# Chunk 0 of two attention backwards in 16 visits of three key blocks, and one weight fetch in five parts

## The chip, the cores and the metric

One NeuronCore of a Trainium2 chip runs the whole program. The metric is device time in microseconds (us), the median of several runs. Its engines are called as in the profile: PE (TensorE, matrix products and transposes), PEld (its weight loads), DVE (VectorE), ACT (ScalarE), POOL (GpSimd) and SP (SyncE, which issues every DMA of this kernel). Each engine works through its own instruction list in order.

## The reference: what is computed

Four layers on an x of 2048 rows by 640 columns in bfloat16: linear attention (A), sliding-window attention (B), A, B, with the same two weight sets used twice, and then the gradients of the whole chain.

```python
x = A_x
x = x + _A_ref(_layernorm(x, axis=-1), A_wqkv, A_wo)
x = x + _B_ref(_layernorm(x, axis=-1), B_wqkv, B_wo)
x = x + _A_ref(_layernorm(x, axis=-1), A_wqkv, A_wo)
x = x + _B_ref(_layernorm(x, axis=-1), B_wqkv, B_wo)
```

The outputs are x and the gradients of A_x, A_wqkv, A_wo, B_wqkv and B_wo. B has 32 heads of 20 columns and a causal window of 256 rows:

```python
scores = jnp.einsum("bhqd,bhkd->bhqk", q, k) * (Dh ** -0.5)
mask = (idx[:, None] - idx[None, :] >= 0) & (idx[:, None] - idx[None, :] < W)
p = _softmax(jnp.where(mask[None, None], scores, -1e9), axis=-1)
```

The change lies in the backward of B, for layer 3 and for layer 1.

## The kernel before

The program runs in passes: the forward of all layers, the backward of layer 3 (B), of layer 2 (A), of layer 1 (B), of layer 0 (A), and products for the weight gradients that are spread over the end. A pass is written out by hand: the order of the calls in Python is the order on PE, DVE, ACT and POOL, and in the two B backwards on SP too.

**Chunks, slabs and visits.** `core` (L1382) does a B backward in eight chunks of 256 query rows (two tiles of 128). A chunk has four slabs (`qr`, eight heads each), loaded by `core_loads` (L1341): slabT and slabqT (transposed k, v and q) and slabks and slabqs (k and q by rows). slabqT and slabqs have two buffers each. A slab has two halves (`p`), and `core_visits` (L708) cuts the blocks of a half into three visits. A block is one pair of a query tile and a key tile, 128 by 128, for one group of heads, two heads at a time. Chunks 1 to 7 have twelve blocks in a half, four in each visit. Chunk 0 has no keys before it and only six blocks, so two in each visit; 24 visits in every chunk.

**What a visit does.** `core_visit` (L759) works on four visits at once, six deep (`st.lag`): for visit n it forms the scores s on PE and e = exp(s) on ACT (L788) and masks e on POOL (L803 for two diagonal blocks in one instruction, L807 for one block); for visit n-3 it forms dp on PE and ds = dp * e on DVE (L792); for visit n-4 it transposes ds on PE (L814) and copies it out as dsT on ACT (L819) or DVE (L821); for visit n-6 `core_acc` accumulates on PE and, in the last visit of a half, the sums leave on ACT (L873, L881) and DVE. Ahead of the transposes of ds stand a number of transposes of the identity, whose result nobody reads (`warm`, L218), called warm-ups here: eight or nine in chunk 0 and five in chunk 1 by the list `thin`. s and dp have one PSUM tile each: the next s waits for e, the next dp for ds.

**What is laid between.** Each visit has two places for a piece of other work. `plan_before` prepares the next chunk (loads gb and ob, transposes gb on PE at L207, multiplies by WoTB, folds on POOL at L921 and L923, transposes into dT at L941). Its times are in a unit of which 32 make 24 visits; the chunk before gives it the room. `plan_behind` finishes a chunk two chunks later and first reads the tile WTB there, and WoTA after it. `hooks` are calls at the start of a visit, hook k at visit int(0.75 k); in layer 3 the first seven hold the end of the forward, hook 20 fetches WTB (the transposed qkv weights of B, 2400 KB) and hook 40 WoTA (800 KB). Layer 1 reads the same two tiles again.

**SP.** `put` hands a DMA over with a delay in visits, and `tick` issues what is due; the delays only set the order on SP. At run time SP issues the next DMA as soon as the one before is issued and its own data and buffer are free. In the first visit of each slab the loads of its slabks and slabqs are handed over with delay 1, and slabqT and slabT of the next slab with 1.1 and 1.3, so the order on SP is slabks, slabqs, slabqT, slabT.

Of the kernel before, what the change touches and what calls it, by code (L numbers as in the profile page):

```python
# [16 lines left out]
D = 640  # L17
# [58 lines left out]
class Kern:  # L76
# [119 lines left out]
            else:  # L196
                self.after(i, first)

    def fetch(self, w, src):
        self.dma(w.rearrange("p a b -> p (a b)"), src)  # L200

    def flip(self, ps, sb, src, name, w, n, step, eng, cols=None, **kw):

# [504 lines left out]
    def core_visits(self, st, l, S, c, qr, dq):  # L708

        t0 = 2 * c  # L710
        w0 = max(t0 - 2, 0)
        for p in range(2):
            if c == 0:
                order = [[(0, 0), (1, 0), (1, 1)]] * 2
            else:
                order = [[(0, 0), (0, 1), (1, 1), (0, 2), (1, 2), (1, 3)], [(0, 0), (0, 1), (0, 2), (1, 2), (1, 3), (1, 1)]]
            units = [(gi, bi, kk) for gi in range(2) for bi, kk in order[gi]]
            m = len(units) // 3
            for v in range(3):
                class U:  # L720
                    pass
                u = U()
                u.c, u.qr, u.p, u.S, u.dq, u.t0, u.w0, u.m = c, qr, p, S, dq, t0, w0, m
                u.blocks = units[v * m:(v + 1) * m]
                u.runs = []
                for j, (gi, bi, kk) in enumerate(u.blocks):
                    if u.runs and u.runs[-1][0:2] == [gi, bi] and u.runs[-1][2] + u.runs[-1][4] == kk and w0 + kk != t0:
                        u.runs[-1][4] += 1
                    else:
                        u.runs.append([gi, bi, kk, j, 1])  # L730
                u.first, u.last = v == 0, v == 2
                u.n = 24 * c + 6 * qr + 3 * p + v
                u.by_dma = self.by_dma(u.n)
                yield u

# [6 lines left out]
    def order(n):  # L742

        return ("FPA", "PFA", "PAF", "FAP", "AFP", "APF")[PLACES["fo"][n % 24] if 48 <= n < 192 else 0]

    WARM = (8, 5)
    TAIL = 5

# [10 lines left out]
    def core_visit(self, st, l, u, piece, on_act, thin):  # L759

        nc = self.nc
        h = st.hist
        h.append(u)

        def back(n):
            return h[-1 - n] if len(h) > n else None
        d, f, a = back(3), back(4), back(st.lag)
        pairs = []
        if d is not None:
            assert all(R["ok"] == at for R, at in d.S["ring"])  # L770
            d.dp = st.pD.tile([P, 2, 512], F32, name="dp")
            pairs.append(self.core_pairs(d, d.dp, lambda gi, bi: d.S["dT"][bi][:, 2 * d.qr + gi, :], "vT"))
        if u is not None:
            s = st.pS.tile([P, 2, 512], F32, name="s")
            pairs.append(self.core_pairs(u, s, lambda gi, bi: u.S["qT"][:, bi, gi, :], "kT"))
        if len(pairs) == 2:
            x, y = pairs
            while x or y:
                for z in (x, y):
                    if z:  # L780
                        z.pop(0)[1]()
        elif pairs:
            for _, z in pairs[0]:
                z()
        if u is not None:
            w = u.m * P
            u.e = st.pe.tile([P, 2, 4 * P], BF, name="e")
            nc.scalar.activation(u.e[:, :, 0:w], s[:, :, 0:w], ACT.Exp)  # L788
        if d is not None:
            w = d.m * P  # L790
            d.ds = st.pd.tile([P, 2, 4 * P], BF, name="ds")
            nc.vector.tensor_tensor(out=d.ds[:, :, 0:w], in0=d.dp[:, :, 0:w], in1=d.e[:, :, 0:w], op=ALU.mult)  # L792
            d.dsT = st.pt.tile([P, 8, P], BF, name="dsT")
            if d.by_dma:
                self.put(14, d.dsT, d.ds.rearrange("p j k -> p (j k)"), transpose=True)
        if u is not None:
            eb = u.e.rearrange("p j (k q) -> p j k q", q=P)
            for far in (0, 1):
                js = [j for j, (gi, bi, kk) in enumerate(u.blocks) if u.w0 + kk == u.t0 + bi - 2 * far]
                kw = dict(compare_op=ALU.is_ge, fill=0.0, base=-far, channel_multiplier=-1 if far else 1)  # L800
                if js == [0, 2]:
                    v = u.e.rearrange("p j (k q) -> p (j k) q", q=P)[:, 0:8:2, :]
                    nc.gpsimd.affine_select(out=v, in_=v, pattern=[[0, 4], [1 if far else -1, P]], **kw)  # L803
                    continue
                for j in js:
                    v = eb[:, :, j, :]
                    nc.gpsimd.affine_select(out=v, in_=v, pattern=[[0, 2], [1 if far else -1, P]], **kw)  # L807
        def flip_ds():
            ps = st.ps.tile([P, 8, P], BF, name="flip", tag="m")
            if thin:  # L810
                self.warm(thin, ps)
            for j in range(2):
                for i in range(f.m):
                    nc.tensor.transpose(ps[:, 4 * j + i, :], f.ds[:, j, i * P:(i + 1) * P], self.ident)  # L814

            def v(t):
                return t.rearrange("p (a b) q -> p a b q", a=2)[:, :, 0:f.m, :]
            if on_act:
                nc.scalar.copy(v(f.dsT), v(ps))  # L819
            else:  # L820
                nc.vector.tensor_copy(v(f.dsT), v(ps))  # L821
        parts = dict(F=None if f is None or f.by_dma else flip_ds, P=piece[0], A=None if a is None else lambda: self.core_acc(st, l, a))
        self.tick(0.5)
        for k in self.order(len(h) - 1):
            if parts[k] is not None:
                parts[k]()
        if piece[1] is not None:
            piece[1]()
        self.tick(0.5)
# [552 lines left out]
    def core(self, st, l, g_out, B, hooks):  # L1382
# [3 lines left out]
        plan = []  # L1386
        dq = {}
        for c in range(1, NC):
            plan += [(32 * (c - 1) + a, *f) for a, *f in self.plan_before(st, l, c, B)]
        for c in range(NC):  # L1390
            plan += [(32 * (c + 2) - (16 if c == NC - 1 else 0) + a, *f)
                     for a, *f in self.plan_behind(st, l, c, dq, g_out)]
        nv = 24 * NC + st.lag
# [7 lines left out]
        for n in range(48):  # L1401
            thin[n] = PLACES[f"ws{l}"][n] if n < 12 else self.WARM[n // 24]
        for n in range(168, nv):
            thin[n] += PLACES["tt"][n - 168]
        on_act = [PLACES["xx"][n % 24] for n in range(nv)]
        n = 0
        with ExitStack() as es:
            st.pS = self.pool(es, "pS", 1, bass.MemoryType.PSUM, "right")
            st.pD = self.pool(es, "pD", 1, bass.MemoryType.PSUM, "right")
            st.hist = []  # L1410
            for c in range(NC):
                for qr in range(4):
                    S = B.slabs.pop(0)
                    for i, u in enumerate(self.core_visits(st, l, S, c, qr, dq)):
                        for k, f in enumerate(hooks):
                            if int(k * 0.75) == n:
                                f()
                        if i == 0:
                            S["late"]()
                        if i == 0 and 4 * c + qr + 1 < 4 * NC:  # L1420
                            B.slabs.append(self.core_loads(l, *divmod(4 * c + qr + 1, 4), B))
                        if n == st.lag:
                            st.pA = self.psum(es, "pA", 1)
                            dqp = self.pool(B.dqs, "dqp", 3, side="right")
                        if n % 24 == st.lag:
                            dq[c] = dqp.tile([P, 2, QT], BF, name="dq")
                        self.core_visit(st, l, u, slots[n], on_act[n], thin[n])
                        n += 1
            for _ in range(st.lag):
                self.core_visit(st, l, None, slots[n], on_act[n], thin[n])  # L1430
                n += 1
# [14 lines left out]
    def passes(self):  # L1446
# [5 lines left out]
        st = S()  # L1452
        with ExitStack() as rest:
# [9 lines left out]
            hooks = tail[:-1] + [lambda: (tail[-1](), switch())] + [lambda: None] * (7 - n3)  # L1463

            hooks += [lambda: None] * (70 - len(hooks))
            hooks[20] = lambda: self.fetch(st.WTB, self.WT["B"])
            hooks[40] = lambda: self.fetch(st.WoTA, self.WoT["A"])
            left3 = self.core(st, 3, self.gs[2], st.core, hooks)
            for f in left3[:8]:
                if f is not None:  # L1470
# [10 lines left out]
            lp, B = self.linear_pools(lw, "left", 0), S()  # L1481
# [8 lines left out]
            plan = [(a, lambda f=f: f and f()) for a, f in enumerate(left3)] + [(20, next_pools)]  # L1490
# [16 lines left out]
            hooks = self.slots([(a - 20, f) for a, f, *_ in fs if a >= 20], 8)  # L1507
# [60 lines left out]
            with ExitStack() as es, ExitStack() as le:  # L1568
# [8 lines left out]
                X, plan = {}, []  # L1577
# [79 lines left out]
```

## Time and profile before

| | us |
|---|---|
| median of three runs | 2156.81 |
| lowest and highest run | 2153.57 and 2165.6 |
| profiled execution, first to last instruction | 2161.7 |
| TensorE busy in it | 2022.5 (94%) |
| VectorE, ScalarE, GpSimd busy | 1396.7, 1313.6, 1034.4 |

The profiled execution has no time of its own beside its span; the span lies within the three timed runs. In the lines further down a group reads: line of the kernel, engine, operation, tiles written and read, count, busy time and mean of one instruction, and idle time ahead with what ended it. In a line of the timeline the first two numbers are the start and the duration in us, and the bracket holds the idle time before it and its releaser. For a DMA on SP the duration is that of the issue; the time to landing is listed apart.

### The profile page before, as it was taken

Reading aid. Unit: us, or ns where it says so; the run is one execution under the profiler, and the core shown is the slowest. Engines: PE = TensorE matmul, PEld = TensorE weight load, DVE = VectorE, ACT = ScalarE, POOL = GpSimd, SP = SyncE. Lnnn points to the kernel's source line nnn. Section 1 sums busy time; section 2 is a strip of 40 time slices with the busy share of each in tenths; the row PEclk is TensorE's granted clock in tenths of the full one; section 3 lists DMA queues with packets and bytes.
Section 4 is the critical chain, followed back from the end, with each engine's and each line's share of the span. In section 5 each row is a group of like instructions: output and inputs, shape, how many; then the busy total and the mean of one; then the engine's idle time right before and its main releaser. Section 6 shows DMA issues by size and latency. Waiting matters only on the chain.

```text
span 2161.7 us, 77035 instructions
## 1 busy us (share of the span) xinstructions
PE 2022.5 (94%) x32885; PEld 1566.0 (72%) x32885; DVE 1396.7 (65%) x2828; ACT 1313.6 (61%) x1866; POOL 1034.4 (48%) x1643
## 2 busy tenths in 40 slices
PE   8989998899988999999989999999998989999999
PEld 6667776677766877777768778777776888888644
DVE  7788886788854888888748769888886233320000
ACT  6558887478875787777637667777775133330000
POOL 1046666156666577777524466777765211220000
PEclk9999999999998999999989989999999999999999
DMA  7597876699984379988889824899888899989650
GB/s 253 195 230 205 215 203 174 199 228 213 221 204 135 94 160 189 189 191 180 185 269 265 213 82 102 191 191 191 177 181 204 272 296 250 267 203 276 194 164 21
DMA packets 658937, 425.46 MB, mean 197 GB/s; under 512 B 399264, under 2 KB 629408, under 8 KB 658208
## 3 DMA queue, kind: packets, MB, share of 16 engines
q1 hardware_dynamic: 658592, 420.52, 76.7%
q8 instruction: 257, 4.21, 0.8%
q14 instruction: 88, 0.72, 0.1%
HBM read 195.17 MB, written 144.70 MB: 157 GB/s over the span
## 4 chain that ended last, share of the span: by engine, by line
PE 51%; DVE 8%; DMA 7%; ACT 6%; issue 4%; POOL 3%; SPq 2%; DVEq 0%; ACTq 0%; POOLq 0%
PE dense L187 17%; PE wg L187 14%; DVE ds L792 5%; PE acc L187 4%; PE dp L187 3%; PE flip L207 3%; PE flip L814 2%; DMA pqb<-pqk 2%; SPq L131 2%; ACT e L788 2%; PE flip L218 1%; PE sT L187 1%; PE ops L187 1%; ACT eT L450 1%; ACT dsT L819 1%
## 5 line engine op out<-in xcount | busy, mean ns | idle before, releaser
L792 DVE TENSOR_TENSOR ds<-dp,e 128x1024 bf16<-128x1024 f32 (+1 forms) x384 | 444.0, 1156 | 122.0 <-PE s L187 76.7
L788 ACT ACTIVATE e<-s 128x1024 bf16<-128x1024 f32 (+1 forms) x384 | 375.0, 976 | 113.5 <-PE s L187 94.9
L450 ACT ACTIVATE eT<-sT 128x2048 bf16<-128x2048 f32 x180 | 338.3, 1880 | 94.9 <-PE sT L187 77.9
L187 PE MATMUL wg<-rhs,lhs 128*128 128x240 bf16 (+3 forms) x2880 | 372.2, 286 | 4.4 <-DMA lhs<-o 4.4
L187 PEld LDWEIGHTS <-lhs 128*128 128x128 bf16 x2880 | 261.4, 98 | 92.3 <-DMA lhs<-o 5.4
L807 POOL TENSOR_SCALAR_AFFINE_SELECT e<-e 128x256 bf16<-128x256 bf16 x512 | 207.5, 420 | 166.7 <-ACT e L788 163.4
L187 PEld LDWEIGHTS <-dqT 128*128 128x128 bf16 x1920 | 174.0, 98 | 61.5 <-issue 4.4
L458 POOL TENSOR_SCALAR_AFFINE_SELECT eT<-eT 128x512 bf16<-128x512 bf16 x256 | 163.8, 644 | 107.1 <-ACT eT L450 103.2
L187 PE MATMUL acc<-slabqs,ds 128*128 128x20 bf16 x2880 | 195.9, 172 | 2.6 <-ACT dq L876 0.3
L187 PE MATMUL acc<-ds,e 128*128 128x20 bf16 x2880 | 193.6, 171 | 0.0
L187 PEld LDWEIGHTS <-ds 128*128 128x128 bf16 x2880 | 173.3, 96 | 19.7 <-issue 15.3
L187 PE MATMUL dp<-slabT,dT 32*128 32x128 bf16 (+1 forms) x1952 | 150.0, 244 | 28.5 <-DVE ds L792 22.6
L803 POOL TENSOR_SCALAR_AFFINE_SELECT e<-e 128x512 bf16<-128x512 bf16 x224 | 143.3, 640 | 60.0 <-ACT e L788 57.8
L187 PEld LDWEIGHTS <-e 128*128 128x128 bf16 x2880 | 164.3, 96 | 5.8 <-issue 1.5
L1304 DVE CAST wr<-wg 128x240 bf16<-128x240 f32 (+3 forms) x54 | 24.5, 453 | 221.7 <-PE wg L187 215.6
L187 PE MATMUL dense<-WB,hnT 128*128 128x320 bf16 x960 | 161.8, 303 | 1.2 <-ACT hnT L210 0.7
L1196 POOL TENSOR_TENSOR dh<-dh,lg 128x640 f32<-128x640 f32 x32 | 46.0, 1438 | 241.7 <-DVE s L1193 219.1
L187 PE MATMUL dense<-WTA,dqT 128*128 128x320 bf16 x960 | 156.3, 299 | 2.5 <-DMA dqT<-dqa 2.2
L1302 ACT CAST wr<-wg 128x240 bf16<-128x240 f32 (+3 forms) x36 | 14.3, 397 | 236.8 <-PE wg L187 234.2
L814 PE MATMUL flip<-ident,ds 128*128 128x128 bf16 x1920 | 153.4, 221 | 3.4 <-DVE ds L913 3.4
L187 PE MATMUL dense<-WTB,dqT 128*128 128x320 bf16 x960 | 154.6, 302 | 0.0
L187 PE MATMUL s<-slabT,slabqT 32*128 32x128 bf16 (+1 forms) x1952 | 147.5, 246 | 4.5 <-ACT e L788 4.5
(184 smaller groups left out, 4473.0 us busy)
## 6 DMA issues: line engine op xcount, KB each, us to landing
T<-T SPq DMA_DIRECT2D x96, 256.0 KB, 3.7
s<-s SPq DMA_DIRECT2D x32, 512.0 KB, 3.2
slabT<-T SPq DMA_DIRECT2D x64, 256.0 KB, 3.6
dqkv<-dq SPq DMA_DIRECT2D x16, 960.0 KB, 6.6
dqkv<-dqa SPq DMA_DIRECT2D x32, 480.0 KB, 4.7
rhs<-dqkv SPq DMA_DIRECT2D x32, 480.0 KB, 5.9
rhs<-dqkv SPq DMA_DIRECT2D x16, 960.0 KB, 6.6
hn<-hn SPq DMA_DIRECT2D x64, 160.0 KB, 3.3
```

The source lines that it names most:

```text
L131: return self.nc.sync.dma_start(out=out, in_=in_, transpose=transpose)
L187: return self.nc.tensor.matmul(out, lhsT=lhsT, rhs=rhs, start=start, stop=stop, skip_group_check=True, **kw)
L207: self.nc.tensor.transpose(t[0:w, j, :], src[:, c0:c0 + w], self.ident)
L450: nc.scalar.activation(e, s, ACT.Exp)
L458: nc.gpsimd.affine_select(out=e, in_=e, compare_op=ALU.is_ge, fill=0.0, base=0, pattern=[[0, 4], [1, P]], channel_multiplier=-1)
L788: nc.scalar.activation(u.e[:, :, 0:w], s[:, :, 0:w], ACT.Exp)
L792: nc.vector.tensor_tensor(out=d.ds[:, :, 0:w], in0=d.dp[:, :, 0:w], in1=d.e[:, :, 0:w], op=ALU.mult)
L803: nc.gpsimd.affine_select(out=v, in_=v, pattern=[[0, 4], [1 if far else -1, P]], **kw)
L807: nc.gpsimd.affine_select(out=v, in_=v, pattern=[[0, 2], [1 if far else -1, P]], **kw)
L814: nc.tensor.transpose(ps[:, 4 * j + i, :], f.ds[:, j, i * P:(i + 1) * P], self.ident)
L1196: nc.gpsimd.tensor_tensor(out=x["dh"], in0=x["dh"], in1=L["g"][:, i, :], op=ALU.add)
L1304: nc.vector.tensor_copy(o[:, 0:w], ps[:, 0:w])
```

## The change

In chunk 0 of both layers each half is cut into two visits of three blocks. The eight visits that go are the first eight numbers: the chunk starts at number 8 (`V0`), so that every later visit keeps its number and its entries in the lists. The pieces of `plan_before` for chunk 1 are squeezed into the sixteen visits that remain. The hooks count from the new first visit. WTB is fetched in five parts of three tiles each (480 KB), at hooks 24, 30, 36, 42 and 48, and WoTA at hook 54.

```diff
-    def fetch(self, w, src):
-        self.dma(w.rearrange("p a b -> p (a b)"), src)
+    def fetch(self, w, src, a=0, b=None):
+        b = w.shape[1] if b is None else b
+        self.dma(w[:, a:b].rearrange("p a b -> p (a b)"), src[:, a * D:b * D])
...
-            m = len(units) // 3
-            for v in range(3):
+            nv = 3 if c else 2
+            m = len(units) // nv
+            for v in range(nv):
...
-                u.first, u.last = v == 0, v == 2
-                u.n = 24 * c + 6 * qr + 3 * p + v
+                u.first, u.last = v == 0, v == nv - 1
+                u.n = 24 * c + 6 * qr + 3 * p + v if c else self.V0 + 4 * qr + 2 * p + v
...
+    V0 = 8
...
-        for k in self.order(len(h) - 1):
+        for k in self.order(self.V0 + len(h) - 1):
...
-            plan += [(32 * (c - 1) + a, *f) for a, *f in self.plan_before(st, l, c, B)]
+            for a, *f in self.plan_before(st, l, c, B):
+                if c == 1:
+                    a = self.V0 / 0.75 + a * (1 - self.V0 / 24) if a < 32 else a
+                plan.append((32 * (c - 1) + a, *f))
...
-        n = 0
+        n = self.V0
...
-                            if int(k * 0.75) == n:
+                            if int(k * 0.75) + self.V0 == n:
...
-                        if n == st.lag:
+                        if n == self.V0 + st.lag:
...
-                        if n % 24 == st.lag:
+                        if n == (24 * c or self.V0) + st.lag:
...
-            hooks[20] = lambda: self.fetch(st.WTB, self.WT["B"])
-            hooks[40] = lambda: self.fetch(st.WoTA, self.WoT["A"])
+            for k in range(5):
+                hooks[24 + 6 * k] = lambda k=k: self.fetch(st.WTB, self.WT["B"], 3 * k, 3 * k + 3)
+            hooks[54] = lambda: self.fetch(st.WoTA, self.WoT["A"])
```

## The prediction, on record before the result

> **What bounds the kernel now.** I read the page first (parts 1 and 4), then the windows of the first chunk of each attention backward, then the timeline of TensorE inside one of them.
>
> ```profile
> span 2161.7 us, 77035 instructions
> PE 2022.5 (94%) x32885; PEld 1566.0 (72%) x32885; DVE 1396.7 (65%) x2828; ACT 1313.6 (61%) x1866; POOL 1034.4 (48%) x1643
> PE 51%; DVE 8%; DMA 7%; ACT 6%; issue 4%; POOL 3%; SPq 2%; DVEq 0%; ACTq 0%; POOLq 0%
> ```
>
> TensorE is busy 94% and carries half of the chain, so time that leaves PE's queue usually leaves the end. But the change touches only two short stretches, chunk 0 of layer 3 (from 665.4 us) and of layer 1 (from 1238.6 us), so I ask what ends last there. The columns are: window and length, busy time of PE, PEld, DVE, ACT and POOL, granted clock, DMA share, GB/s.
>
> ```profile
> 665.40:690.50 25.10, 20.32 (x294) 14.52 (x293) 11.99 (x24) 11.14 (x20) 11.94 (x23) 0.76 0.32 98
> 692.00:708.00 16.00, 15.88 (x368) 14.26 (x369) 11.03 (x21) 11.76 (x24) 6.81 (x18) 1.00 0.77 271
> 707.60:719.60 12.00, 11.00 (x229) 8.91 (x222) 8.21 (x12) 10.22 (x18) 6.18 (x13) 1.00 0.48 148
> 1238.60:1248.60 10.00, 4.65 (x38) 2.59 (x37) 1.64 (x5) 5.99 (x10) 8.33 (x12) 0.61 0.46 133
> 1248.60:1263.90 15.30, 15.04 (x249) 11.84 (x249) 9.65 (x19) 7.20 (x14) 10.47 (x19) 0.81 0.13 36
> 1263.90:1280.40 16.50, 16.50 (x384) 14.85 (x384) 11.84 (x22) 12.04 (x25) 7.62 (x19) 1.00 0.40 122
> ```
>
> The reader should see two regimes. Each chunk opens with a start that waits, at a low granted clock (0.76 and 0.61). After it PE is full (15.88 of 16, 16.50 of 16.50) while ACT has over a quarter free. In that second part PE's own work sets the time. This is one of its visits:
>
> ```profile
> 696.33 0.23 PE L187 MATMUL dp<-slabT,dT 32*128 32x128 bf16 x2
> ...
> 696.55 0.62 PE L218 MATMUL flip<-ident 128*128 128x128 bf16 x8
> 697.01 0.39 PE L814 MATMUL flip<-ident,ds 128*128 128x128 bf16 x4
> 697.23 0.17 PE L187 MATMUL acc<-slabqs,ds 128*128 128x20 bf16 x1
> ...
> 697.61 0.28 PE L187 MATMUL dp<-slabT,dT 32*128 32x256 bf16 x2
> ```
>
> From start to start: s and dp 0.22 us, eight warm-up transposes 0.46, the four transposes of ds 0.22, 24 small acc products 0.38: 1.28 us. The warm-ups (L218) belong to the visit, not to its blocks. That is what the change can win.
>
> **The change, part by part.**
>
> *Warm-ups.* A visit of three blocks keeps its eight, and the rest grows by half: 0.33 + 0.46 + 0.33 + 0.57 = 1.69 us. Two of these replace three of 1.28, so 3.38 for 3.84. How many warm-ups there are now, per layer:
>
> ```profile
> L218 PE MATMUL flip<-ident x166: 216/219/230, 677.8 to 707.9; 128*128 128x128 bf16 x166
> L218 PE MATMUL flip<-ident x160: 219/219/314, 1249.0 to 1279.7; 128*128 128x128 bf16 x160
> ```
>
> The first window already holds five of chunk 1, so 161 and 160. Afterwards the first four visits have nothing to transpose and the other twelve have eight: 96 each. So 65 + 64 = 129 go, at 0.46/8 = 0.0575 us: **-7.4 us**. This is the largest term, and a hard one, as nothing beside PE hides them in the full stretches.
>
> *Other engines, at nothing.* Per layer 24 exponentials of 128x512 become 16 of 128x768, likewise the products ds and the copies dsT; 32 masks of 128x256 become 16 of 128x512; 32 of the s and dp matmuls merge with a neighbour, with the same columns. The small and the large forms stand here:
>
> ```profile
> L792 DVE TENSOR_TENSOR ds<-dp,e x384: 680/1225/1226, 676.0 to 1651.9; 128x1024 bf16<-128x1024 f32 x168, 128x512 bf16<-128x512 f32 x24
> L788 ACT ACTIVATE e<-s x384: 597/1024/1105, 665.8 to 1645.9; 128x1024 bf16<-128x1024 f32 x168, 128x512 bf16<-128x512 f32 x24
> L803 POOL TENSOR_SCALAR_AFFINE_SELECT e<-e x224: 632/637/1219, 709.6 to 1648.2; 128x512 bf16<-128x512 bf16 x112
> ...
> 696.82 0.69 DVE L792 TENSOR_TENSOR ds<-dp,e 128x512 bf16<-128x512 f32 x1 [0.25 <-PE s L187]
> ```
>
> 128x768 has no row; it lies between the two, 0.60 to 1.02 on ACT and 0.68 to 1.23 on DVE, and I take the middles, 0.81 and 0.95. In the visit above ds starts 0.49 after the first dp (696.82 less 696.33), with a third block 0.60, and ends at 1.55 of 1.69, so the next dp, which needs the bank, is not held. At the upper end (1.23) it would be held 0.14 per visit, at most 2.8 us in the ten full visits of each layer. The cover is PE itself; a faster PE would expose DVE next.
>
> *The start.* Pieces for chunk 1 are squeezed from 24 visits into 16, so they come earlier counted in visits. In layer 3 the first transposes of gb move from the second visit into the first:
>
> ```profile
> 665.71 1.03 PE L941 MATMUL flip<-ident,ds 128*128 128x128 bf16 x8
> 666.67 0.39 PE L187 MATMUL s<-slabT,slabqT 32*128 32x128 bf16 x4
> 670.91 0.71 PE L207 MATMUL flip<-ident,gb 128*128 128x128 bf16 x5 [3.85 <-DMA gb<-in_grad_out_dram]
> ```
>
> PE waits there until 670.9 for the load of gb, whose issue does not move. The L941 group and the second s, 1.35 us at half clock, now run behind that wait instead of before it. Queued behind the waiting transpose are all later s, so ACT, too. Cost 0 (if they fall into later gaps) to +1.4; I take +0.9. In layer 1 DVE's first ds waits until 1247.92 for a store, and PE with it; pieces that come earlier fall into that hole, such as this dense group:
>
> ```profile
> 1247.92 0.69 DVE L792 TENSOR_TENSOR ds<-dp,e 128x512 bf16<-128x512 f32 x1 [7.94 <-DMA g<-lgn]
> 1251.98 1.54 PE L187 MATMUL dense<-WoTB,gT 128*128 128x320 bf16 x5
> ```
>
> It moves from the sixth visit to the fourth: 0 to -2.2 with the gb transposes that move along, taken as -1.5. Together **-0.6**, ends -2.2 and +1.4.
>
> *Slabs.* This is the new wait. slabqs has two buffers, and the buffer is free only six visits after the slab's last visit. A slab now lasts four visits, so the slabqs of the third and fourth slab of chunk 0 and of the first of chunk 1 wait for an acc that is one visit away, and behind them in SP's queue stand the slabqT and slabT that the *next* slab's first s needs.
>
> ```profile
> 690.09 0.25 PE L187 MATMUL acc<-slabks,dsT 128*128 128x20 bf16 x4
> ...
> 690.24 0.37 SPq L131 DMA_DIRECT2D slabqs<-s  x1
> 690.67 0.46 SPq L131 DMA_DIRECT2D slabqT<-T  x1
> 691.17 0.43 SPq L131 DMA_DIRECT2D slabT<-T  x1
> ```
>
> So slabT is issued 0.93 us after the acc. Now that acc is followed by six visits before the slab is wanted; afterwards by two (3.38 us, and 3.83 the second time, with a dT transpose of 0.45 between). The slab after that, the second of chunk 1, again has four. With L to land, PE stalls 0.93 + L - 3.38 and 0.93 + L - 3.83. The nine issues of slabT from 660 to 760 us landed in (smallest, median, largest):
>
> ```profile
> DMA to landing us min/median/max: 2.7/3.4/5.1
> ```
>
> So L is 2.7 to 5.1; I take 3.5, near its median: 1.05 + 0.6 per layer, **+3.3**; at 2.7 it is 0.5, at 5.1 it is 9.7.
>
> *Into chunk 1.* Six visits of three blocks, instead of two, are still to be accumulated when it starts: per layer 6 blocks of acc (0.19 each), four of transposes (0.11), three of dp (0.05), 1.7 us of PE work that I counted as moved, not gone. The window 707.6 to 719.6 has 1.0 us of PE free, so up to 1.0 of it is absorbed; against that three wider dsT copies (0.2 more each, as for e) on a nearly full ACT (10.22 of 12) may add 0.6. Taken as **0**, ends -2.0 and +1.2 for both layers.
>
> *The fetches.* One issue of 2400 KB becomes five of 480, and WoTA goes from the 31st visit to the 41st.
>
> ```profile
> WTB<-WTBt SPq DMA_DIRECT2D x1, 2400.0 KB, 11.4
> L187 PE MATMUL dense<-WTB,dqT x960: 296/299/474, 777.1 to 1685.3; 128*128 128x320 bf16 x192
> 708.23 1.64 SPq L131 DMA_DIRECT2D slabT<-T  x1
> 718.89 0.28 PE L187 MATMUL s<-slabT,slabqT 32*128 32x256 bf16 x2
> ```
>
> Today it runs beside a PE that is full, so nothing is won by splitting it. The parts sit between the third and the 21st visit of chunk 1, well before the first use at 777. SP gets four more issues of about 0.4 us; a slab in chunk 1 is issued 10.7 us before its s (708.23 to 718.89), and one part holds the DMA engines 11.4/5 = 2.3 us. **0**; without that cover 5 x 2.3 = 11.4.
>
> Sum: -7.4 - 0.6 + 3.3 + 0 + 0 = **-4.7 us**. Against the profiled execution 2161.7 becomes 2157.0. That execution lies inside the three timed runs shown (2153.57 to 2165.6), so I carry the difference to their median: 2156.8 - 4.7 = **2152.1 us**.
>
> **The rivals.**
>
> *Quick (0.22).* Slabs land in 2.7 us as the quiet rows say, start and chunk 1 take their good ends: -7.4 - 2.2 + 0.5 - 2.0 = -11.1, 2145.7. For it: DMA share between slabs is low in layer 1 (0.13). Against: the start of layer 3.
>
> *Late slabs (0.12), slower than before.* The stalls are 4L - 10.7 in sum (with L over 2.9); the rest of the sum is -8.0; so the change loses from L = 4.7 on. At the row's maximum of 5.1 it ends 1.7 us slower, 2158.5. The maximum was seen while the big WTB transfer ran, and that moves away: against.
>
> *Late slabs and a lost clock (0.06).* The window around the 3.85 us hole shows a granted clock of one half:
>
> ```profile
> 665.40:674.00 8.60, 4.49 (x35) 2.83 (x34) 1.24 (x3) 3.40 (x5) 1.58 (x4) 0.50 0.54 172
> ```
>
> PE ran slowly for some 7 us after it, 3.5 us lost. Four stalls that each did so add 14: 2172. Against: stalls of at most 2.65 us are shorter than any hole seen here with that result. The Trainium skill, page "TensorE: Matmul & The Clock Gate", section "HAM oscillation", puts the danger at PE gaps over about 3.4 us; the 3.85 us hole agrees (though the eight transposes of L941 took 1.03 us, not 0.62, before it already), no gap near 2 us in these windows tests it, and by that rule this case is nothing.
>
> *Exposed parts (0.06), slower too.* If each part of WTB holds up a slab fully: -4.7 + 11.4, 2163.5. It needs a slab to lose more than 5.6 us of lead (10.7 less the longest landing, 5.1); one part takes 2.3. The Trainium skill, page "DMA: Bandwidth & Descriptors", section "Bandwidth", speaks for this rival: it asks for batches of 1 MiB or more, and the parts are below half of that; by it the fetch is dearer in sum and the time leans to this rival's. The only row here is 2400 KB in 11.4 us; none shows the split.
>
> *It does nothing (0.06).* The warm-ups only filled waits, and chunk 0 stays as long: 2157. The rows of 15.88 in 16 speak against it.
>
> **How the numbers follow.** The forecast has 0.48, 2147 to 2158. All bounds together go from -11.1 to +7.7, 2145.7 to 2164.5; with some 3 us below for a median of three runs that spread by 12, and without the topmost part, which needs every bad end at once, 2143 to 2163. That leaves out the lost clock, most of the exposed parts and the edges of the others. 0.5% (10.8 us) is about what a measurement of this kernel can tell from no change. Faster than 2146.0: most of the quick case (0.14) and the forecast's edge (0.06), 0.20. Slower than 2167.6: the lost clock and the tops of the other slow cases, 0.11. Within: 0.69.
>
> **What would show it.** The first s of chunk 0 and of chunk 1 in either layer now:
>
> ```profile
> 665.38 0.39 PE L187 MATMUL s<-slabT,slabqT 32*128 32x128 bf16 x4
> ...
> 707.34 0.28 PE L187 MATMUL s<-slabT,slabqT 32*128 32x256 bf16 x2
> ...
> 1238.60 0.28 PE L187 MATMUL s<-slabT,slabqT 32*128 32x128 bf16 x4
> ...
> 1280.35 0.28 PE L187 MATMUL s<-slabT,slabqT 32*128 32x256 bf16 x2
> ```
>
> 129 fewer L218 matmuls; full-speed visits of chunk 0 of 1.7 us; that distance 39.1 us in layer 3 (42.0 less 3.7, less 1.7 moved, plus 0.9 and 1.65) and 36.5 in layer 1 (41.8 less 3.7, 1.7 and 1.5, plus 1.65); PE waiting for DMA slabT or slabqT ahead of the 13th and 17th visit, about a microsecond each, with slabqs issued late. Wrong if PE waits for DVE ds in each visit, if those waits pass 2.5 us, or if the clock drops outside the start.

## The result and the profile after

The changed kernel takes 2154.44 us (median of 15 runs, 2145.46 to 2162.66); the kernel before, on the same chips, 2161.98 us (15 runs, 2153.57 to 2168.99). The ratio is 0.9964, with a 95% interval of 0.9951 to 0.9978: 7.8 us faster, between 4.8 and 10.6. Forecast were 4.7 us, and a time of 2152.1, from a median of 2156.8 in the three runs then known. The gain is 0.36%, inside the half per cent named as hard to tell from no change; fifteen runs a side do tell it. The profiled execution went from 2161.7 to 2154.1 us, 7.6 less.

The first lines of the page, and the engines' shares of the chain that ended last:

```profile
span 2154.1 us, 76513 instructions
PE 2013.3 (93%) x32692; PEld 1556.0 (72%) x32692; DVE 1391.5 (65%) x2800; ACT 1310.7 (61%) x1846; POOL 1028.0 (48%) x1611
PE 50%; DVE 7%; ACT 6%; DMA 6%; POOL 5%; issue 4%; SPq 2%; DVEq 0%; ACTq 0%; POOLq 0%
```

TensorE is busy for 9.2 us less (2022.5 to 2013.3), about what the span lost. The page can't say where. For that I cut both traces at the same places: from 0.4 us before the first exponential of chunk 0 to 0.9 before the first of chunk 1, and on to 0.9 before the first of chunk 2, in layer 3 and then in layer 1. First the kernel before, then the changed one (window and length; busy PE, PEld, DVE, ACT, POOL; granted clock; DMA share; GB/s):

```profile
665.42:707.25 41.83, 36.88 (x678) 29.47 (x676) 24.02 (x45) 23.16 (x44) 19.97 (x42) 0.86 0.50 166
707.25:755.65 48.40, 46.44 (x1107) 40.02 (x1107) 41.43 (x55) 37.32 (x53) 29.20 (x58) 1.00 0.28 85
1241.39:1280.26 38.87, 35.77 (x656) 29.01 (x655) 22.18 (x40) 23.50 (x45) 23.74 (x46) 0.83 0.31 93
1280.26:1328.88 48.62, 46.23 (x1108) 39.95 (x1107) 41.34 (x55) 37.34 (x53) 29.21 (x58) 1.00 0.23 68
```

```profile
668.84:706.44 37.60, 31.01 (x533) 23.66 (x529) 20.76 (x31) 20.88 (x32) 17.16 (x26) 0.83 0.34 102
706.44:755.76 49.32, 47.80 (x1150) 41.34 (x1150) 42.48 (x55) 38.34 (x55) 29.50 (x58) 1.00 0.45 146
1239.04:1271.91 32.87, 29.59 (x509) 22.60 (x508) 18.89 (x26) 21.27 (x33) 21.05 (x30) 0.84 0.32 91
1271.91:1321.21 49.30, 47.79 (x1150) 41.34 (x1150) 42.47 (x55) 38.34 (x55) 29.48 (x58) 1.00 0.27 79
```

Read the second column. Chunk 0 lost 4.2 us in layer 3 and 6.0 in layer 1; chunk 1 gained 0.9 and 0.7. That is 8.6 us less in the four windows. Outside them the program is the same and differs by single executions: this one came to layer 3's chunk 0 3.4 us later (668.84 against 665.42) and took 2.5 less between the windows of the two layers (755.65 to 1241.39 before, 755.76 to 1239.04 after); what follows layer 1's chunk 1 is alike to 0.1. So -8.6 + 3.4 - 2.5 + 0.1 = -7.6. Over all the profiles of this study the first window begins between 662.4 and 668.8 us though the code ahead of it was the same in each. So a total from one profile is good to some us only; a chunk's length is the sharper instrument, and I use it beside the interval of the timed runs.

A full-speed visit of the changed kernel, the warm-ups' counts and the waits of TensorE from 684 to 706 us:

```profile
689.22 0.23 PE L187 MATMUL dp<-slabT,dT 32*128 32x128 bf16 x2
...
689.50 0.62 PE L219 MATMUL flip<-ident 128*128 128x128 bf16 x8
689.96 0.50 PE L817 MATMUL flip<-ident,ds 128*128 128x128 bf16 x6
690.29 0.17 PE L187 MATMUL acc<-slabqs,ds 128*128 128x20 bf16 x1
...
690.82 0.23 PE L187 MATMUL dp<-slabT,dT 32*128 32x128 bf16 x2
```

```profile
689.64 0.81 ACT L791 ACTIVATE e<-s 128x768 bf16<-128x768 f32 x1 [0.82 <-PE s L187]
689.66 0.96 DVE L795 TENSOR_TENSOR ds<-dp,e 128x768 bf16<-128x768 f32 x1 [0.21 <-PE s L187]
```

```profile
L219 PE MATMUL flip<-ident x96: 219/219/230, 684.1 to 705.5; 128*128 128x128 bf16 x96
L219 PE MATMUL flip<-ident x96: 219/219/314, 1248.5 to 1271.0; 128*128 128x128 bf16 x96
```

```profile
PE s L187 <- DMA slabT<-T: 0.7, 1, 0.7
```

The visit takes 1.60 us (689.22 to 690.82), and ds ends at 690.62 (689.66 + 0.96), 0.20 ahead of the next dp. There are 96 warm-ups per layer, as counted. From 684 to 706 us TensorE waits once for a slab and never for ds.

### The profile page after: what moved, and what is told of

Same layout as the page of the kernel before. It is cut to its first block, busy times and chain, and to the rows that moved or that the text cites. A ratio compares the mean times of both kernels' runs of the same rounds, so it can differ in the third digit from the quotient of the medians.

```text
span 2154.1 us, 76513 instructions
## 1 busy us (share of the span) xinstructions
PE 2013.3 (93%) x32692; PEld 1556.0 (72%) x32692; DVE 1391.5 (65%) x2800; ACT 1310.7 (61%) x1846; POOL 1028.0 (48%) x1611
## 4 chain that ended last, share of the span: by engine, by line
PE 50%; DVE 7%; ACT 6%; DMA 6%; POOL 5%; issue 4%; SPq 2%; DVEq 0%; ACTq 0%; POOLq 0%
PE dense L187 18%; PE wg L187 15%; DVE ds L795 5%; PE acc L187 4%; PE dp L187 3%; PE flip L208 2%; DMA pqb<-pqk 2%; PE flip L817 2%; ACT e L791 2%; SPq L131 2%; PE sT L187 1%; POOL e L810 1%; PE ops L187 1%; ACT eT L451 1%; DMA dsT<-ds 1%
## 5 line engine op out<-in xcount | busy, mean ns | idle before, releaser
L810 POOL TENSOR_SCALAR_AFFINE_SELECT e<-e 128x256 bf16<-128x256 bf16 x448 | 182.2, 422 | 139.2 <-ACT e L791 139.0
L806 POOL TENSOR_SCALAR_AFFINE_SELECT e<-e 128x512 bf16<-128x512 bf16 x256 | 163.2, 639 | 90.5 <-ACT e L791 87.2
```

## The experiments

My theory after the result: fewer warm-ups on a full TensorE bring the gain, the slabs cost about a microsecond, and splitting the fetch brings nothing. A rival: the warm-ups only filled waits and something else in the wider visit brought the gain. In each experiment the whole time is set against the kernel before on the same chip. Chunk 0 is told as "layer 3 / layer 1", from first exponential to first exponential: 42.3 / 39.4 before, 38.1 / 33.4 after.

**1. The kernel before with as few warm-ups as the changed one (96 per layer).**

```diff
-            thin[n] = PLACES[f"ws{l}"][n] if n < 12 else self.WARM[n // 24]
+            thin[n] = (5 if n < 20 else 4) if n < 24 else self.WARM[n // 24]
```

> The kernel before, 24 visits of two blocks in chunk 0, but with 96 warm-up transposes per layer there instead of 161 and 160 (nothing else; the arithmetic is untouched). Theory W (the gain is the PE time of 129 warm-ups): 7.4 us faster than before, about as fast as the change; chunk 0, from its first e to the first e of chunk 1, 42.3 to about 38.6 us in layer 3 and 39.4 to about 35.7 in layer 1. Theory L (a visit is held by the chain dp to ds to the next dp: 0.49 + 0.69 + about 0.1 us is already 1.28, so the warm-ups only fill a wait, and three blocks share one such chain): at most 2 us faster, full visits stay at 1.2 to 1.28 us, and PE then waits for DVE ds in most visits.

Measured: 2155.25 against 2158.53 us, ratio 0.9989 (0.9974 to 1.0005). Chunk 0 40.7 / 37.1: 3.9 us less in sum, between the two theories: not the 7.4 of the pure price, and more than the 2 at most of a chain that covers them all. Here is a visit of it:

```profile
693.78 0.23 PE L187 MATMUL dp<-slabT,dT 32*128 32x128 bf16 x2
...
694.00 0.45 PE L218 MATMUL flip<-ident 128*128 128x128 bf16 x5
...
694.27 0.69 DVE L792 TENSOR_TENSOR ds<-dp,e 128x512 bf16<-128x512 f32 x1 [0.25 <-PE s L187]
...
695.01 0.28 PE L187 MATMUL dp<-slabT,dT 32*128 32x256 bf16 x2
```

From dp to dp 1.23 us, where the visit with eight took 1.28. Three warm-ups went, 0.17 us, and 0.05 came of it. The rest is the chain beside TensorE: ds begins 0.49 after dp, takes 0.69, and 0.05 later the next dp has its bank: 0.49 + 0.69 + 0.05 = 1.23. In the two-block visit this chain stood almost level with TensorE's own work: 0.12 of the 0.17 us of warm-ups taken out had only covered it. Once per layer the chain is longer, as ds also needs the masked e. There GpSimd was late with the masks, and TensorE stood still for 0.98 us:

```profile
687.75 0.69 DVE L792 TENSOR_TENSOR ds<-dp,e 128x512 bf16<-128x512 f32 x1 [1.47 <-POOL e L807]
...
688.50 0.23 PE L187 MATMUL dp<-slabT,dT 32*128 32x128 bf16 x2 [0.98 <-DVE ds L792]
```

That visit takes 2.23 us, 0.55 more than in the kernel before, and its counterpart in layer 1 0.33 more. Over both chunks about half of the price of the warm-ups was paid out. The same chain in the wider visit is 0.44 + 0.96 = 1.40 us, for three blocks, under 1.60.

**2. The changed kernel with as many warm-ups as before (160 per layer).**

```diff
+            thin[n] = (13 if n < 20 else 14) if n < 24 else self.WARM[n // 24]
```

> The change with the removed warm-ups put back (13 or 14 in a visit instead of 8, 160 per layer). Theory W: the gain is gone, within 2 us of before, full visits 1.60 + 5.3 x 0.0575 = 1.9 us. Theory L: the same, since PE becomes longer than the chain of 1.6 us; a run that stays 5 us or more faster than before speaks against both and for another source of the gain.

Measured: 2159.30 against 2158.53 us, ratio 1.0002 (0.9987 to 1.0017). Chunk 0 41.0 / 36.8: 6.3 us more than in the changed kernel for 128 warm-ups, 49 ns each. The gain is gone. One slab is late in layer 1, none in layer 3:

```profile
1273.92 0.23 PE L187 MATMUL s<-slabT,slabqT 32*128 32x128 bf16 x2 [0.83 <-DMA slabT<-T]
```

The wider visit alone is worth little: chunk 0 is 3.9 us shorter than before in sum, 3.4 of which is work moved to chunk 1, by the prediction's count, where 1.7 come back (49.4 / 49.3 for 48.4 / 48.6). Experiments 1 and 2 are two edges of a square: fewer warm-ups alone 3.9 us, wider visits alone about 2.2, both 8.6. The two need each other.

**3. The changed kernel with the fetch in one piece, where it was before.**

```diff
-            for k in range(5):
-                hooks[24 + 6 * k] = lambda k=k: self.fetch(st.WTB, self.WT["B"], 3 * k, 3 * k + 3)
-            hooks[54] = lambda: self.fetch(st.WoTA, self.WoT["A"])
+            hooks[20] = lambda: self.fetch(st.WTB, self.WT["B"])
+            hooks[40] = lambda: self.fetch(st.WoTA, self.WoT["A"])
```

> The change with WTB fetched in one piece at hook 20 and WoTA at hook 40, as before. If the fetch is hidden, as the prediction has it: within 2 us of the change. Rival: the one fetch of 2400 KB (11.4 us to land) now stands ahead of the slab that chunk 1 begins with, which has only two visits of lead; then PE waits for that slab some 4 to 8 us once, in layer 3 alone, at the first visit of chunk 1.

Measured: 2159.05 against 2158.53 us, ratio 1.0012 (0.9993 to 1.0031). Chunk 0 is unchanged (38.4 / 33.0), chunk 1 of layer 3 takes 55.8 us instead of 49.3. The size is the one expected, the victim is not: it isn't a slab but the gb of chunk 2. First SP's queue, then TensorE:

```profile
698.84 0.44 SPq L131 DMA_DIRECT2D WTB<-WTBt  x1
699.32 0.43 SPq L131 DMA_DIRECT2D gb<-in_grad_out_dram  x1
```

```profile
709.53 0.71 PE L208 MATMUL flip<-ident,gb 128*128 128x128 bf16 x5 [5.30 <-DMA gb<-in_grad_out_dram]
```

gb is issued 0.48 us behind the 2400 KB and is wanted 4.9 us later; TensorE stands still for 5.30 us. The granted clock (third number from the end) falls to one half in the middle of this hole, at 707.0, and stays there until 713.8, so the transposes behind it run slowly too:

```profile
707.10:713.70 6.60, 4.17 (x77) 3.55 (x78) 0.96 (x1) 3.00 (x6) 1.00 (x2) 0.50 0.57 183
```

In the changed kernel the parts are issued from 711.5 us on, take 4.6 us each to land (median), and nothing waits for them. So the second half of the change wins nothing by itself but keeps 6.5 us, in this profile, from being lost by the first; the timed runs, 1.0012 here and 0.9964 for the changed kernel, point the same way. Two things were put back at once, the size and the place; which of them alone would do was not tried. The Trainium skill, page "DMA: Bandwidth & Descriptors", section "Bandwidth", asks for batches of 1 MiB or more; here the transfer above that size cost 6.5 us through what was queued behind it, and the parts below it cost nothing.

**4. The kernel before with the fetch in five parts.** Its edit is the two parts of the diff that touch the fetch, and nothing else.

> The kernel before with only the second part of the change: WTB in five parts at hooks 24 to 48 and WoTA at hook 54. Prediction's step (hidden either way, nothing won): within 2 us of before, chunks 0 and 1 of both layers as before (42.3 and 48.4, 39.4 and 48.6 us). Rival (the one fetch of 2400 KB delays the load of gb here too): chunk 1 of layer 3 gets shorter by a microsecond or more.

Measured: 2160.14 against 2156.55 us, ratio 1.0010 (0.9992 to 1.0027). Chunk 0 41.0 / 39.4, chunk 1 48.4 / 48.6. Only layer 3's start moved, by 1.3 us, with a granted clock of 0.72 instead of 0.62 in its first 16 us: the stretch at half clock lasted 13.7 us there, and 17.1 in the kernel before. The fetch isn't in that stretch, so I count it to the spread of executions. Splitting wins nothing where nothing waited.

**5. The changed kernel with a third buffer for slabqs.**

```diff
-            q = B.slab.tile([P, 1, 2, 2, P], BF, name="slabqs", bufs=2)
+            q = B.slab.tile([P, 1, 2, 2, P], BF, name="slabqs", bufs=3)
```

> The change with three buffers for slabqs instead of two, so that SP no longer waits for an acc one visit away and slabT is issued early. Prediction's step: the slab waits go, 3.3 us by the prediction, 0.9 by the profile after (one wait of 0.7 and a late start of the weights at the 13th visit of layer 3, none in layer 1). PE waits for no DMA slabT or slabqT in chunk 0; chunk 0 of layer 3 38.1 to about 37.3 us, layer 1 unchanged at 33.4. Rival: the wait only hid another (ACT behind the accumulators), then chunk 0 of layer 3 stays at 38.1.

Measured: 2150.32 against 2158.53 us, ratio 0.9967 (0.9953 to 0.9980). Chunk 0 37.4 / 32.6, that is 0.7 and 0.8 less than with two buffers, and no wait of TensorE for a slab. Layer 1 was expected unchanged; of its 0.8 us, 0.30 stands at the 13th visit and 0.52 in the start, where no wait for a slab is seen. Chunk 1 of layer 3 takes 0.35 us longer (49.7), with a wait of 0.6 for ds. The total can't tell this from the changed kernel (0.9964); the chunks can. The wait that goes is this one, of the changed kernel (SP's queue, then TensorE, then the landing of that one slabT and of the next):

```profile
694.57 0.37 SPq L131 DMA_DIRECT2D slabqs<-s  x1
694.99 0.46 SPq L131 DMA_DIRECT2D slabqT<-T  x1
695.50 0.43 SPq L131 DMA_DIRECT2D slabT<-T  x1
```

```profile
698.45 0.23 PE L187 MATMUL dp<-slabT,dT 32*128 32x128 bf16 x2
699.35 0.23 PE L187 MATMUL s<-slabT,slabqT 32*128 32x128 bf16 x2 [0.67 <-DMA slabT<-T]
```

```profile
DMA to landing us min/median/max: 3.7/3.7/3.7
...
DMA to landing us min/median/max: 2.8/2.8/2.8
```

slabqs waits for its buffer until 694.57; slabT stands 0.93 us behind it, lands 3.7 after that, and s, due 3.88 us after 694.57, is late by 0.93 + 3.7 - 3.88 = 0.75 (0.84 by the length of that visit against the one with three buffers). The next slab lands in 2.8 and isn't late. It is the mechanism of the prediction, at one place per layer instead of two.

**6. The changed kernel with three warm-ups a visit instead of eight,** and the same with the third buffer.

```diff
+            thin[n] = 3 if n < 24 else self.WARM[n // 24]
```

> The change with 3 warm-ups instead of 8 in each visit of chunk 0 (120 fewer in all, the arithmetic untouched). Theory W (PE's own work bounds a visit of three blocks): full visits 1.60 to 1.31 us, 6.9 us or more faster than the change, chunk 0 38.1 to 34.6 and 33.4 to 29.6 us. Theory L (after the change PE and the chain dp to ds to the next dp are about level; the chain is 0.44 + 0.96 + 0.1 = 1.50 us): visits stop at about 1.5 us, chunk 0 loses 1 to 1.5 us per layer beside what the slow start saves (two visits at half clock in layer 1, about 1 us), 2 to 4 us in all, and PE waits for DVE ds or ACT e in most visits. Both: the clock stays at 1.00 after the start, or the gain turns into a loss.

> The change with three buffers for slabqs and 3 warm-ups in chunk 0: the version that the runs so far point to. If the slab wait returns with shorter visits (two visits of 1.5 instead of 1.8 us until the slab is wanted), the third buffer is worth more here than the 0.7 us that it was in layer 3 of the change: 1 to 2 us per layer against the run with 3 warm-ups alone. In all 10 to 13 us faster than before. If PE's work were the only bound, as theory W has it, 15 us or more.

Measured: 2149.02 against 2156.55 us, ratio 0.9963 (0.9948 to 0.9978), chunk 0 36.1 / 34.1; with the third buffer 2148.72 (6 runs) against 2156.55, ratio 0.9959 (0.9944 to 0.9974), chunk 0 35.3 / 30.3. With the third buffer the gain is 8.8 us by the ratio (5.6 to 12.1), where 10 to 13 were expected. With two buffers, in layer 3, 60 warm-ups fewer give 2.0 us of the 3.5 at 0.0575 each. The slab's wait only moved, from the 13th visit to the other place that the prediction named, the 17th (0.75 us by the length of that visit, after 0.84), and ds is late once:

```profile
PE s L187 <- DMA slabT<-T: 1.0, 1, 1.0
PE dp L187 <- DVE ds L795: 0.5, 1, 0.5
```

```profile
703.81 0.23 PE L187 MATMUL s<-slabT,slabqT 32*128 32x128 bf16 x2 [1.00 <-DMA slabT<-T]
```

Without the slab, five of the twelve visits with warm-ups became 0.25 to 0.28 us shorter, four 0.08 to 0.16, and three not at all. What holds each of these seven was not told apart.

Layer 1 got slower, with two buffers: TensorE's clock fell in the middle of a nearly full stretch. These are windows of that execution:

```profile
1255.60:1257.80 2.20, 2.20 (x64) 1.94 (x61) 1.73 (x3) 1.50 (x3) 2.20 (x4) 1.00 0.03 7
1257.80:1260.00 2.20, 1.94 (x43) 1.50 (x39) 1.28 (x3) 2.20 (x5) 1.76 (x4) 1.00 0.44 120
1260.00:1262.20 2.20, 2.05 (x44) 1.70 (x42) 1.73 (x3) 1.39 (x3) 1.16 (x2) 0.71 0.60 178
1262.20:1264.40 2.20, 2.20 (x39) 1.76 (x39) 0.99 (x2) 1.66 (x4) 0.72 (x2) 0.50 0.04 7
...
1268.80:1271.00 2.20, 2.20 (x43) 1.87 (x41) 0.94 (x2) 1.76 (x2) 0.07 (x1) 0.50 0.98 327
```

In the granted clock, the third number from the end, 1.00 becomes 0.50 while TensorE is busy 1.94 and 2.05 of 2.20 us.

**7. Both of these kernels once more,** to see whether the clock falls each time.

> The kernel with 3 warm-ups once more, for one profile. In its first profile layer 1 lost the clock in the middle of chunk 0 (granted 0.50 from about 1261 to 1271 us, visits of 2.0 to 2.9 us, chunk 0 34.1 us) without a PE gap of half a microsecond, while layer 3 kept it. If the loss belongs to the kernel (too little PE work in a window where SP's slab wait and ACT hold it), layer 1 shows it again at the same visits. If it hangs on where a free-running window of the clock falls, this profile shows it elsewhere or not at all, and chunk 0 of layer 1 takes about 30 to 31 us.

> The kernel with 3 warm-ups and three slabqs buffers once more, for one profile. Its first showed chunk 0 at 35.3 and 30.3 us with a clock of 1.00 after the start. The same again (within 0.5 us in each layer, but for the start) if the third buffer is what keeps PE full enough for the clock; a lost clock of 3 us or more in one of the layers if it was luck.

Measured, one run each beside a run of 2155.37 us of the kernel before: 2149.10 and 2142.97 us. Chunk 0 36.0 / 31.0 and 35.2 / 30.9, at a granted clock of 0.83 in layer 1's chunk 0 both times (0.70 in the execution above). So this kernel also runs without the fall; whether it comes depends on the execution. In these two profiles three warm-ups are worth 2.1 and 2.3 us per layer over the changed kernel, and the third buffer 0.8 and 0.1 beside them. By chunk 0 the version with both is the best, 2.5 to 3.1 us per layer below the changed kernel in its two profiles; it is faster than the kernel before, while against the changed kernel the timed runs, on different chips, can't tell.

## Why the prediction was right, and which terms were off

The direction, the place and the mechanisms held, but for the reason given for the warm-ups; the sum came out 3.9 us too small against the windows (-4.7 forecast, -8.6 measured). That the time itself came within 2.3 us of the 2152.1 forecast is partly luck: the median of the kernel before rose by 5.2 us from three runs to fifteen, and the larger gain made up about 3 of it. From the first s of chunk 0 to that of chunk 1 it is 37.8 and 35.7 us, where 39.1 and 36.5 were forecast. Term by term:

| term | forecast | measured | by |
|---|---|---|---|
| warm-ups, 129 fewer | -7.4 | -6.3 | experiment 2, 49 ns each |
| start of the two chunks | -0.6 | -1.6 | what is left of chunk 0's change |
| slabs | +3.3 | +1.1 | visits beside those of experiment 5 (1.5 by its chunks) |
| into chunk 1 | 0 | -1.8 | 3.4 moved, 1.6 come back |
| other engines, fetches | 0 | 0 | the visit; experiment 4 |

Waits for slabs are mixed into the first two rows: experiment 2 had 0.83 us of them in layer 1 and none in layer 3, the changed kernel 0.30 and 0.84. With these taken out, the warm-ups come to -6.6 (52 ns each) and the start to -1.3.

*Warm-ups.* The size is nearly right, the reason for calling it certain was not: "a hard one, as nothing beside PE hides them". In the kernel before, the chain from dp by ds to the next dp hid about half of them, as experiment 1 shows. The prediction looked at the chain of the wide visit (ds ends at 1.55 of 1.69) and not at that of the narrow one, where the same sum, 0.49 + 0.69 of 1.28, left 0.1. That the whole price was paid out is owed to the wider visit, which moves the chain's fixed 0.44 to 0.49 us from every two blocks to every three. Had the change only thinned the warm-ups, the same argument would have forecast twice what came.

*Other engines.* Right to a hundredth: e of 128x768 takes 0.81, ds 0.96 for 0.81 and 0.95. The visit takes 1.60 for 1.69: acc 0.53 for 0.57, dp and s 0.28 for 0.33. The merged dp and s, which I had let grow by half, grow by less.

*Slabs.* The term with the largest error. The mechanism is the one described (slabqs waits, the rest of SP's queue stands behind it, TensorE waits at the 13th visit). L of 3.5 was fair for the first of the two in layer 3 (3.7) and high for the other three (3.0, 2.8 and 2.9), and the lead was 3.88 us, not 3.38: of the two visits in between, one ends a half and takes longer, with the accumulators leaving through ACT ahead of its e. I had priced both as full visits. So the wait is 0.84 in layer 3, 0.30 in layer 1, and none at the 17th visit. Where a slab is late differs between executions, as experiments 2 and 6 show. The rival "late slabs" needed L = 4.7; the longest of these four was 3.7.

*Into chunk 1.* The work moved came back by half; the value of 0 stood between -2.0 and +1.2, and -1.8 is close to the good end. Chunk 1 had more room than the 1.0 us I read from one window of 12: TensorE was busy 46.4 of 48.4 us of it.

*The start.* A remainder, with the errors of the other terms in it. Without the slabs' waits it is about -1.7 in layer 1, where -1.5 was forecast, and +0.3 in layer 3 instead of +0.9. In layer 3 the wait for gb stays, and the group that I had put behind it (ds, eight transposes) does run behind it, in the changed kernel:

```profile
674.22 0.72 PE L208 MATMUL flip<-ident,gb 128*128 128x128 bf16 x5 [5.02 <-DMA gb<-in_grad_out_dram]
674.73 1.06 PE L944 MATMUL flip<-ident,ds 128*128 128x128 bf16 x8
```

So the step happened as told, and +0.9 was too high a point of 0 to +1.4; why it cost less was not measured. Part of layer 1's gain is the clock's: eight warm-ups take 1.03 us at half clock and 0.62 at full, and 8 of them stand at half clock where 18 stood before. Half clock covers 10.2 us of layer 1's chunk 0, in the kernel before 12.6.

```profile
1248.53 1.03 PE L219 MATMUL flip<-ident 128*128 128x128 bf16 x8
...
1251.90 0.62 PE L219 MATMUL flip<-ident 128*128 128x128 bf16 x8
```

*The clock.* In the changed kernel it is at 1.00 in both chunks 1, and in the chunks 0 it is lower in the starts alone, as the prediction asked. But the rival "late slabs and a lost clock" read layer 3's start wrongly. It tied the half clock to the hole of 3.85 us, though it saw slow transposes ahead of it. In the kernel before, the clock was at one half from 660.5 us on, and the hole began at 667.06:

```profile
657.10:660.50 3.40, 1.96 (x49) 1.37 (x45) 1.18 (x3) 1.74 (x2) 3.32 (x7) 0.99 0.16 53
660.50:663.90 3.40, 2.50 (x41) 2.31 (x42) 0.00 (x0) 1.80 (x2) 3.40 (x7) 0.50 0.00 0
```

In the 3.4 us ahead of that fall no idle time of TensorE was longer than 0.51 us.

*The other rivals.* "Exposed parts" is out, as nothing waits for a part; but a part lands in 4.6 us, not in the 2.3 of DMA time that I gave it, so the lead was used more than I thought. "It does nothing" is out for the change and half true for the kernel before. "Quick" (-11.1) is as near to the timed -7.8 as the forecast is (3.3 and 3.1 off), and nearer to the -8.6 of the windows: it had slabs and chunk 1 close to where they came out, and the warm-ups too dear.

What stays open: whether the fetch's size or its place protects chunk 1, and why an execution of the same code differs by several us outside these chunks, so that the timed runs spread by 17 us. The runs themselves give a hint: time and mean granted clock go together. Of the changed kernel's fifteen runs the three with a clock of 0.975 to 0.977 took 2157.3 to 2162.7 us, the two with 0.983 and 0.984 took 2148.6 and 2145.5 (correlation -0.89). Which of the two drives the other was not tested.

## What to carry to other kernels

Before padding on the bounding engine is priced at its full duration, add up the chain of dependent steps that runs beside it in the same turn: padding that only covers this chain pays nothing when it goes, and a wider turn, which spreads the chain's fixed part over more work, lets it pay. When turns get fewer and wider, count each load's lead again in turns and in microseconds, and look at what a large transfer has queued behind it: a fetch that was harmless in 24 turns cost 6.5 us in 16. And where whole runs spread by more than the effect, compare the length of the stretch that was changed, across several profiles.

## What was not expected of the hardware

TensorE's granted clock fell from 1.00 to 0.50 for 10.2 us (experiment 6) without any long gap. The longest idle time of TensorE in the two windows around the fall is this:

```profile
1258.48 0.23 PE L187 MATMUL s<-slabT,slabqT 32*128 32x128 bf16 x2 [0.20 <-ACT e L791]
```

The prediction had put the danger at holes of 3.85 us, as in layer 3's start. The Trainium skill, page "TensorE: Matmul & The Clock Gate", section "HAM oscillation", puts it at gaps over about 3.4 us. This row doesn't agree, nor does layer 3's start, where the clock fell ahead of the hole; in layer 1 a hole of 3.56 us (kernel before) or 3.33 us (changed kernel) does lie at the fall or just ahead of it.

The eleven traces show a pattern, but not the cause. They hold 151 stretches at half clock, without those in which a program ends: 79 of 3.41 us, 38 of 6.83, 19 of 10.24, and 15 that last longer multiples of 3.41. Within one execution all of them begin on one grid of 3.413 us. A first guess is that the work met this grid in another way when the kernel was run again and kept its clock. The traces speak against that: counted from the first exponential of the chunk, the grid lay within 0.1 us at the same place in both executions, and TensorE did the same work in the step ahead of the fall. First that step and the time after it, then the same step and the next of the execution that kept its clock:

```profile
1257.51:1260.92 3.41, 3.00 (x66) 2.23 (x64) 2.02 (x4) 2.98 (x7) 2.54 (x5) 1.00 0.53 149
1260.95:1271.15 10.20, 10.20 (x167) 8.66 (x165) 6.23 (x8) 6.99 (x12) 2.88 (x6) 0.50 0.40 123
```

```profile
1256.04:1259.45 3.41, 3.00 (x66) 2.23 (x63) 2.02 (x4) 2.98 (x7) 2.46 (x5) 1.00 0.52 160
1259.47:1262.85 3.38, 3.37 (x87) 2.96 (x85) 2.77 (x4) 3.21 (x6) 1.32 (x3) 1.00 0.12 35
```

So neither a gap, nor the place of the grid, nor the busy share of the profile tells the two apart, and the cause of the fall stays open. Of the four profiles with three warm-ups one shows such a fall, and of the three with eight none does. That taking out the last warm-ups leaves a kernel nearer to losing its clock is therefore a guess.
